# Keys pooled by matmuls, and one exponential for eight heads in the first nine chunks

## The chip, the cores and the metric

The kernel runs on one core of one Trainium2 chip. The metric is the device time of one execution in microseconds (us), as the median of three runs. The core has TensorE (PE; PEld is its loading of weights), DVE (VectorE), ACT (ScalarE), POOL (GpSimd) and SP (SyncE), which here issues nearly all loads and stores.

## The reference

Three stages follow each other: attention over pooled keys and values, a layer with a rational activation, and a layer with a squared ReLU. Only the first one is touched by the change.

```python
# q, k, v: (8, 8, 576, 64) float32 = batch, heads, tokens, head size
k_p = k.reshape(B, H, Sp, 8, D).mean(axis=3)      # Sp = 72 pooled keys
v_p = v.reshape(B, H, Sp, 8, D).mean(axis=3)
scores = scale * np.matmul(q, k_p.transpose(0, 1, 3, 2))
scores = scores - np.max(scores, axis=-1, keepdims=True)
attn = np.exp(scores)
attn = attn / (np.sum(attn, axis=-1, keepdims=True) + 1e-09)
x = np.matmul(attn, v_p)          # to (4608, 512): tokens x model
h = x @ w_in                      # 512 -> 2048
g = (a0 + a1*h + a2*h**2 + a3*h**3) / (1 + |b0||h| + |b1|h**2 + 1e-6)
x = g @ w_out                     # 2048 -> 512
y = np.maximum(x @ w_in2, 0.0)
out = y * y @ w_out2              # (4608, 512)
```

## The kernel before

The 4608 tokens (8 batches of 576) are cut into 36 chunks of 128 and nine blocks of 512. A block's four chunks must have gone through attention before the block's first layer can begin, so the first four chunks lie ahead of every large matmul. The work of one chunk is: scores (`qk`), the maximum over the 72 keys of each head (`row_max`), the exponential and its sum (`exps`), the division (`norm`), a transpose of the attention weights (`a_turn` for the first nine chunks), the product with the pooled values (`av`), and the output for the layers as a high and a low part (`x_out`). In the MoE layers every matmul group is 12 products of 128x128 by 128x512.

The first nine chunks (`NF = 9`, batches 0 and 1) use plain float32 attention. Later chunks use split 16-bit operands and are not touched. For the first two batches, keys and values are loaded raw and pooled on the core (`kv_first`). A key load brings one pair of heads as 128 rows (two heads of 64) by 576 tokens; DVE sums each eight neighbours (one reduce from 576 to 72), and ACT scales the result. There are four pairs in a batch. A value load brings 128 tokens by 512 columns, and TensorE sums eight neighbours with a constant 0/1 matrix `sums`, accumulating five chunks of tokens (four of 128 and one of 64) into one PSUM bank.

For each of the first nine chunks the scores of the eight heads stand in two PSUM banks, four heads of one parity in each, called the two halves. Each half has its own maximum on DVE. In half 0 ACT then makes four exponentials, one for each head, that subtract the maximum as a bias and accumulate the sum. In half 1 (named in `WHOLE`) DVE subtracts the maxima of all four heads in one instruction, ACT makes one exponential, and DVE makes one sum. The division is DVE's for chunks 0, 2, 3, 5 and 8 and ACT's, head by head, for the others. After the transposes, DVE evacuates half 0 and ACT half 1; in chunk 1, DVE takes both (`TURN_DVE`).

The order of work is not written by hand. Every operation is put on a list with its engine, an estimated time and its tiles (`act`, `dve`, `pe`, `load`). A planner (`Plan.order`, lines 380 to 401) simulates the list many times with random shifts of the due times, and keeps the order that ends first. Each engine then runs its queue strictly in that order. For loads, the planner also adds a "not before" dependency where it wants one held back. The second batch's pooling may start only when the transposes of chunk 0 have been issued (`plan.after = turned[0]`). As all instructions are issued by one line, 409, the profile names it everywhere; tiles tell the work apart. The names are: `kr` and `vr` raw keys and values (pooled keys lie in the same tiles, those of batch 1 in `vr`), `y`, `sc` and `xp` PSUM banks of attention, `mx`, `e` and `sm` the maxima, exponentials and sums, `t` the transposed weights, `raw` and `w` MoE weights while they are decoded, `x` the input of the layers and `h` a PSUM bank that the value pooling shares with the layers.

Of the kernel before, what the change touches and what calls it, by code (L numbers as in the profile page):

```python
# [17 lines left out]
AF = mybir.ActivationFunctionType  # L18
ALU = mybir.AluOpType
AX = mybir.AxisListType  # L20

B, H, S, D = 8, 8, 576, 64
POOL = 8
SP = S // POOL
NT = B * S
DM = H * D
# [3 lines left out]
TB = 512  # L30
# [26 lines left out]
SCALE = 1.0 / POOL / 8  # L57
# [2 lines left out]
QC = 1.0 + 1e-6  # L60
NF = 9
NORM_DVE = {0, 2, 3, 5} | set(range(8, NCHUNK))
WHOLE = {(c, 1) for c in range(NF)} | {(15, 1)}
TURN_DVE = {(c, 0) for c in range(NF)} | {(1, 1)}
BY_DMA = {(1, 1), (1, 3), (1, 5)}
KA, KB = 128 - SP, 2 * SP - 128
KC = SP + 2 * KB
# [1 line left out]
S0W = S // 128 * (128 // POOL)  # L69
WS = S0W + SP  # L70
NK = NF * CH // S
# [344 lines left out]
def fused_kernel(  # L416
# [1 line left out]
    tc: tile.TileContext,  # L418
    qf: bass.AP,
    qt: bass.AP,  # L420
    kf: bass.AP,
    vn: bass.AP,
    vm: bass.AP,
    kt: bass.AP,
# [41 lines left out]
    def act(n, func, **kw):  # L466
        pointers = sum(isinstance(kw.get(k), View) for k in ("scale", "bias"))
        fixed = (0.05 if kw["in_"].base.psum else 0.093) + (0.3 if "accum_out" in kw else 0.0)
        plan.add("act", fixed + 0.093 * pointers + n / 1200, [(nc.scalar.activation, dict(func=func, **kw))])

    def dve(n, name, **kw):
        pointers = sum(isinstance(kw.get(k), View) for k in ("scalar", "scalar1"))
        fixed = 0.11 if name == "tensor_reduce" else 0.066
        plan.add("dve", max(0.15, fixed + 0.061 * pointers + n / 960), [(getattr(nc.vector, name), kw)])

    def tt(n, out, in0, in1, op):
        dve(n, "tensor_tensor", out=out, in0=in0, in1=in1, op=op)
# [4 lines left out]
    def pe(us, products):  # L482
        return plan.add("pe", us, [(nc.tensor.matmul, p) for p in products])

    def load(n, out, in_, early=None):
        plan.add("sp", 0.6, [(nc.sync.dma_start, dict(out=out, in_=in_))], n / LOAD_RATE, early)
# [19 lines left out]
    def h_bank():  # L506
        h_turn.append(0)
        return ps_h.tile([128, TB], F32, "h", f"h{len(h_turn) % 2}")
# [7 lines left out]
    sums = const.tile([128, WS], F32, "sums")  # L516
# [106 lines left out]
    kst, vst, kp_t, vp_t = {}, {}, {}, {}  # L623
# [18 lines left out]
    def kv_first():  # L642


        k, v = ([p1.tile([128, 4 * TB], F32, n, f"x{o + i}") for i in range(2)] for o, n in ((0, "kr"), (2, "vr")))
        kr = [k[g // 3][:, g % 3 * S:(g % 3 + 1) * S].rearrange("p (k r) -> p k r", r=POOL) for g in range(H // 2)]
        vr = [v[c // 4][0:min(128, S - 128 * c), c % 4 * TB:(c % 4 + 1) * TB] for c in range(5)]
        for b, t in enumerate((k, v)):
            o = 1024 if b else S
            kp_t[b] = t[1][:, o:o + H // 2 * SP].rearrange("p (g k) -> p g k", g=H // 2)  # L650
            vp_t[b] = t[1][0:SP, 1536:2048]

        def k_sum(b):
            plan.ahead = K_AHEAD if b == 0 else 0.0
            for g in range(H // 2):
                load(128 * S * 4, kr[g], kf[b, g].rearrange("p (k r) -> p k r", r=POOL))
                dve(S, "tensor_reduce", out=kp_t[b][:, g], in_=kr[g], axis=AX.X, op=ALU.add)
                act(SP, AF.Copy, out=kp_t[b][:, g], in_=kp_t[b][:, g], scale=SCALE)
            if b == 0:
                q_first(0)  # L660

        def v_sum(b):
            plan.ahead = AHEAD if b == 0 else 0.0
            ps = h_bank()[0:SP]
            for c in range(5):
                n, o = min(128, S - 128 * c), S0W - 16 * c
                load(n * TB * 4, vr[c], vn[b, :, TB * c:TB * (c + 1)] if c < 4 else vm[b])
                pe(1.0, [dict(
                    out=ps, lhsT=sums[0:n, o:o + SP], rhs=vr[c], start=(c == 0), stop=(c == 4),
                )])  # L670
            act(DM, AF.Copy, out=vp_t[b], in_=ps)
            if b == 0:
                q_first(2)
                q_first(3)

        k_sum(0)
        plan.ahead = AHEAD
        q_first(1)
        v_sum(0)
        for c, fn in ((K1C, k_sum), (V1C, v_sum)):  # L680
            at(starts[c] + 5 if c >= 0 else -S0, "t", fn, 1)
# [26 lines left out]
    def q_first(c):  # L708

        if c == 0:  # L710
            q_in[0] = p1.tile([128, 4, 4, CH], F32, "q", "w7")
        q_t[c] = q_in[0][:, c]
        load(128 * 4 * CH * 4, q_t[c], qf[c])
# [76 lines left out]
    def row_max(c, half):  # L790
        if half == 0:
# [6 lines left out]
            H // 2 * SP, "tensor_reduce", out=mx, in_=sc_t[c, half], axis=AX.X, op=ALU.max,  # L798
            negate=(c, half) not in WHOLE,
        )  # L800

    def exps(c, half):
        mx, sm, e = e_t[c]
        ps = sc_t.pop((c, half))
        hs = slice(half * (H // 2), (half + 1) * (H // 2))
        if (c, half) in WHOLE:
            n = H // 2 * SP
            tt(n, e[:, hs], ps, mx[:, hs].unsqueeze(2).to_broadcast([128, H // 2, SP]), ALU.subtract)
            act(n, AF.Exp, out=e[:, hs], in_=e[:, hs])
            dve(n, "tensor_reduce", out=sm[:, hs], in_=e[:, hs], axis=AX.X, op=ALU.add)  # L810
            return
        for hh in range(H // 2):
            h = half * (H // 2) + hh
            act(
                SP, AF.Exp, out=e[:, h, :], in_=ps[:, hh, :],
                bias=mx[:, h:h + 1], accum_out=sm[:, h:h + 1],
            )
# [11 lines left out]
    def a_turn(c):  # L829
# [4 lines left out]
        for half in range(2):  # L834
# [13 lines left out]
            o = t[:, half * (H // 2):(half + 1) * (H // 2)]  # L848
            if (c, half) in TURN_DVE:
                dve(TB, "tensor_copy", out=o, in_=ps)  # L850
# [380 lines left out]
    def at(slot, key, fn, *args):  # L1231
        todo.setdefault((slot, key), []).append((fn, args))

    def run(slot, key):
        for fn, args in todo.pop((slot, key), []):
            if args and args[0] in FIRST and fn in (k_add, v_add, q_load, qk, row_max, exps, norm, a_turn, av, x_out):
                plan.ahead = AHEAD
            if fn not in (w_raw, w_decode, w_sums, x_fetch, pair_forms) and slot >= GATED:
                plan.after = started.get(slot - WINDOW)
            if fn.__name__ in ("k_sum", "v_sum"):  # L1240
                plan.after = turned.get(K1C if fn.__name__ == "k_sum" else V1C)
            fn(*args)
            plan.ahead, plan.after = 0.0, None

    def place_chunk(c, t):
        if c >= 4:
            at(t - 2, "t", q_load, c)
        at(t, "t", q_split, c)
        for half in range(2):
            h = half if c < CPB else 0  # L1250
            at(t + 2 + h, "s", qk, c, half)
            at(t + 2 + h, "s", row_max, c, half)
            at(t + 2 + h, "s", exps, c, half)
        at(t + 4, "t", norm, c)
        at(t + 5, "t", a_turn if c < NF else a_split, c)
        if c not in TWOS:
            cs = [x for x in (c - 1, c) if x == c or x in TWOS]
            at(t + 6, "x", av, *cs)
            for x in cs:
                at(t + 7, "s", x_out, x)  # L1260
# [63 lines left out]
    setup()  # L1324
    plan.ahead = AHEAD
    kv_first()
    plan.ahead = 0.0
    load_consts()
    for i in range(-S0, N + LAG):
# [11 lines left out]
        m = i - LAG  # L1341
# [5 lines left out]
        if kind == "pair":  # L1347
            _, pair, k = slots[i]
# [54 lines left out]
```

## Time and profile before

| | |
|---|---|
| time, median of 3 runs | 1650.77 us (1649.82 to 1654.72) |
| time of the profiled execution | 1649.59 us |
| its span in the trace | 1647.9 us |
| PE busy | 1610.9 us, 98% |
| PEld busy | 1307.3 us, 79% |
| DVE busy | 1410.0 us, 86% |
| ACT busy | 1132.6 us, 69% |
| mean granted TensorE clock | 0.996 |

Busy times are those of one profiled execution. The span goes from the first to the last instruction; the execution's own time includes what lies around it. A matmul of float32 operands appears as two records in the trace. Matmuls are pipelined, so that a busy PE need not be a PE at its peak.

### The profile page before, as it was taken

To read this page: it belongs to the slowest core of one execution; us is meant where nothing else is said; L and a number is where in the kernel's file an instruction comes from. 1 tells how busy PE (TensorE), PEld (TensorE's weight loads), DVE (VectorE), ACT (ScalarE), POOL (GpSimd) and SP (SyncE) were. 2 spreads that over 40 slices of the span, in tenths; PEclk is the share of its full clock that TensorE was granted. 3 is DMA by queue.
4 is the path that set the end of the run, shared out by engine and by line. 5 is a ranking of instruction groups with operands and counts; after the bars stand their busy time and mean duration, and the time that the engine had idled before them with its cause. 6 is when DMAs were issued, how large, how long until landed. Compare 5 with 4: busy or idle time off the path is not lost.

```text
span 1647.9 us, 23637 instructions
## 1 busy us (share of the span) xinstructions
PE 1610.9 (98%) x8476; PEld 1307.3 (79%) x8476; DVE 1410.0 (86%) x2135; ACT 1132.6 (69%) x2105; POOL 77.8 (5%) x95
## 2 busy tenths in 40 slices
PE   7899999999999999999999999999999999999998
PEld 4678888888888877877787878887888788888886
DVE  7999998589889998488979788999889799996666
ACT  5989778787557766566787645667987466657553
POOL 0001100100001000001111000010000000000000
PEclk9999999999999999999999999999999999999999
DMA  7357578997999879999999996785799985555544
GB/s 269 131 231 196 152 265 298 241 257 250 313 299 286 289 258 274 322 270 279 258 243 281 283 321 245 233 244 190 227 267 263 292 291 200 185 185 171 191 154 141
DMA packets 199141, 401.43 MB, mean 244 GB/s; under 512 B 68752, under 2 KB 118768, under 8 KB 170864
## 3 DMA queue, kind: packets, MB, share of 16 engines
q1 hardware_dynamic: 188512, 379.76, 70.6%
q0 software_dynamic: 10512, 20.16, 7.8%
q8 instruction: 67, 1.10, 0.3%
q14 instruction: 50, 0.41, 0.1%
HBM read 310.91 MB, written 72.35 MB: 233 GB/s over the span
## 4 chain that ended last, share of the span: by engine, by line
PE 70%; DVE 19%; ACT 4%; DMA 3%; issue 2%; SPq 0%; ACTq 0%; DVEq 0%
PE h L409 30%; PE y L409 22%; DVE pq L409 7%; PE yx L409 7%; PE yz L409 5%; PE hz L409 5%; DVE g L409 3%; DVE sv L409 2%; ACT sv L409 2%; PE xp L409 1%; PE sc L409 1%; DMA xd<-xo 1%; DMA t<-a 1%; DVE t L409 1%; DVE wv L409 1%
## 5 line engine op out<-in xcount | busy, mean ns | idle before, releaser
L409 PE MATMUL h<-x,w 128*128 128x512 f32 x2304 | 557.8, 392 | 10.7 <-DVE pq L409 5.1
L409 PEld LDWEIGHTS h<-x,w 128*128 128x128 f32 x2304 | 430.8, 188 | 107.5 <-DVE pq L409 8.9
L409 PE MATMUL y<-g,w 128*128 128x512 f32 x1728 | 418.8, 391 | 3.7 <-DVE g L409 3.6
L409 PEld LDWEIGHTS y<-g,w 128*128 128x128 f32 x1728 | 324.1, 188 | 73.7 <-DVE g L409 6.3
L409 ACT ACTIVATE sv<-sv,cs 128x512 f32<-128x512 f32 x288 | 208.3, 724 | 154.7 <-DVE sv L409 149.8
L409 ACT ACTIVATE sv<-h 128x512 f32<-128x512 f32 x192 | 114.0, 594 | 68.1 <-PE h L409 52.7
L409 PE MATMUL h<-xf,wi 128*128 128x512 f32 x576 | 145.7, 391 | 0.7 <-ACT gb L409 0.5
L409 PE MATMUL yx<-gf,wo 128*128 128x512 f32 x576 | 142.8, 391 | 0.4 <-DVE acc L409 0.4
L409 PE MATMUL y<-w,g 128*128 128x512 f32 x576 | 140.4, 392 | 0.1
L409 ACT ACTIVATE pq<-h,cs 128x512 f32<-128x512 f32 x144 | 111.8, 776 | 24.4 <-PE h L409 14.0
L409 PEld LDWEIGHTS yx<-gf,wo 128*128 128x128 f32 x576 | 107.6, 188 | 24.3 <-issue 0.8
L409 PEld LDWEIGHTS h<-xf,wi 128*128 128x128 f32 x576 | 107.4, 188 | 23.8 <-ACT gb L409 1.4
L409 PEld LDWEIGHTS y<-w,g 128*128 128x128 f32 x576 | 107.2, 188 | 23.3 <-DVE g L409 0.5
L409 DVE SCALAR_TENSOR_TENSOR g<-pq,cs,sv 128x512 fp32r<-128x512 f32 x144 | 107.6, 747 | 19.5 <-ACT sv L409 16.9
L409 DVE SCALAR_TENSOR_TENSOR sv<-sv,cs 128x512 f32<-128x512 f32 x144 | 107.3, 745 | 14.4 <-ACT sv L409 14.3
L409 ACT ACTIVATE sv<-h,cs 128x512 f32<-128x512 f32 x144 | 98.8, 686 | 25.0 <-DVE g L409 15.9
L409 PE MATMUL hz<-xf,wi 128*128 128x512 f32 x432 | 110.2, 392 | 1.8 <-DVE ga L409 1.0
L409 PE MATMUL yz<-gf,wo 128*128 128x512 f32 x432 | 108.3, 392 | 3.1 <-DVE gf L409 1.5
L409 DVE SCALAR_TENSOR_TENSOR pq<-pq,cs 128x512 f32<-128x512 f32 x144 | 107.5, 747 | 1.9
L409 DVE SCALAR_TENSOR_TENSOR pq<-pq,cs,h 128x512 f32<-128x512 f32 x144 | 106.7, 741 | 0.6 <-ACT sv L409 0.2
L409 DVE TENSOR_TENSOR pq<-pq,h 128x512 f32<-128x512 f32 x144 | 98.0, 680 | 8.4 <-ACT pq L409 5.2
L409 DVE SCALAR_TENSOR_TENSOR pq<-sv,g 128x512 f32<-128x512 f32 x144 | 99.1, 688 | 2.8
(147 smaller groups left out, 2072.6 us busy)
## 6 DMA issues: line engine op xcount, KB each, us to landing
w<-ws SPq DMA_DIRECT2D x128, 1024.0 KB, 6.3
ws<-w SPq DMA_DIRECT2D x32, 1024.0 KB, 4.9
wi<-wf SPq DMA_DIRECT2D x48, 512.0 KB, 5.2
wo<-wf SPq DMA_DIRECT2D x48, 512.0 KB, 5.9
wo<-ws SPq DMA_DIRECT2D x72, 256.0 KB, 4.2
raw<-wa SPq DMA_DIRECT2D x16, 1024.0 KB, 6.7
raw<-wb SPq DMA_DIRECT2D x16, 1024.0 KB, 8.1
wf<-ws SPq DMA_DIRECT2D x16, 1024.0 KB, 9.2
```

The lines of the kernel that those rows point to most:

```text
L409: made = fn(**{k: v.real() if isinstance(v, View) else v for k, v in kw.items()})
```

## The change

Keys of the first two batches are pooled by matmuls, as the values are. The host lays out `k` like `v`, so that a load brings 128 tokens (the fifth 64) by 512 columns. For each chunk of tokens and each pair of heads one matmul multiplies 128 columns of raw keys, as the stationary operand, with 16 (in the last chunk 8) columns of the 0/1 matrix, which gives the pooled keys already transposed. They collect in one PSUM bank, and a single ACT instruction scales all 288 columns. The DVE reduces and the four scalings of a batch go.

In the first nine chunks DVE now subtracts the maxima in both halves. After the second half, one exponential and one sum run over all eight heads (576 columns). DVE no longer evacuates transposes of any chunk (`TURN_DVE` is empty); ACT evacuates both halves.

```diff
+MERGED = set(range(NF))
-WHOLE = {(c, 1) for c in range(NF)} | {(15, 1)}
-TURN_DVE = {(c, 0) for c in range(NF)} | {(1, 1)}
+WHOLE = {(c, h) for c in MERGED for h in range(2)} | {(15, 1)}
+TURN_DVE = set()
...
-        kr = [k[g // 3][:, g % 3 * S:(g % 3 + 1) * S].rearrange("p (k r) -> p k r", r=POOL) for g in range(H // 2)]
-        vr = [v[c // 4][0:min(128, S - 128 * c), c % 4 * TB:(c % 4 + 1) * TB] for c in range(5)]
+        kr, vr = (
+            [t[c // 4][0:min(128, S - 128 * c), c % 4 * TB:(c % 4 + 1) * TB] for c in range(5)] for t in (k, v)
+        )
...
-            o = 1024 if b else S
-            kp_t[b] = t[1][:, o:o + H // 2 * SP].rearrange("p (g k) -> p g k", g=H // 2)
+            kp_t[b] = t[1][:, 1024:1024 + H // 2 * SP].rearrange("p (g k) -> p g k", g=H // 2)
...
             plan.ahead = K_AHEAD if b == 0 else 0.0
-            for g in range(H // 2):
-                load(128 * S * 4, kr[g], kf[b, g].rearrange("p (k r) -> p k r", r=POOL))
-                dve(S, "tensor_reduce", out=kp_t[b][:, g], in_=kr[g], axis=AX.X, op=ALU.add)
-                act(SP, AF.Copy, out=kp_t[b][:, g], in_=kp_t[b][:, g], scale=SCALE)
+            ps = h_bank()[:, 0:H // 2 * SP].rearrange("p (g k) -> p g k", g=H // 2)
+            for c in range(5):
+                n = min(128, S - 128 * c)
+                load(n * TB * 4, kr[c], kn[b, :, TB * c:TB * (c + 1)] if c < 4 else km[b])
+                m = n // POOL
+                pe(0.4, [dict(
+                    out=ps[:, g, 16 * c:16 * c + m], lhsT=kr[c][:, 128 * g:128 * (g + 1)],
+                    rhs=sums[0:n, S0W:S0W + m], start=True, stop=True,
+                ) for g in range(H // 2)])
+            act(H // 2 * SP, AF.Copy, out=kp_t[b], in_=ps, scale=SCALE)
...
             tt(n, e[:, hs], ps, mx[:, hs].unsqueeze(2).to_broadcast([128, H // 2, SP]), ALU.subtract)
+            if c in MERGED:
+                if half == 0:
+                    return
+                n, hs = H * SP, slice(0, H)
             act(n, AF.Exp, out=e[:, hs], in_=e[:, hs])
             dve(n, "tensor_reduce", out=sm[:, hs], in_=e[:, hs], axis=AX.X, op=ALU.add)
             return
```

## Rows read from the trace of the kernel before

**Rows 1.** The page: one engine line, and the shares of the chain.

```profile
PE 1610.9 (98%) x8476; PEld 1307.3 (79%) x8476; DVE 1410.0 (86%) x2135; ACT 1132.6 (69%) x2105; POOL 77.8 (5%) x95
...
PE 70%; DVE 19%; ACT 4%; DMA 3%; issue 2%; SPq 0%; ACTq 0%; DVEq 0%
```

**Rows 2.** Stretches: length, busy PE PEld DVE ACT POOL (instructions), clock, DMA, GB/s.

```profile
0.00:40.00 40.00, 28.53 (x213) 17.28 (x214) 28.91 (x60) 23.21 (x69) 1.25 (x8) 0.91 0.78 266
40.00:80.00 40.00, 35.26 (x223) 27.53 (x222) 40.00 (x71) 37.29 (x90) 0.00 (x0) 0.96 0.40 142
80.00:120.00 40.00, 38.81 (x198) 31.03 (x196) 39.38 (x59) 35.58 (x58) 0.00 (x0) 1.00 0.58 231
```

**Rows 3.** The chain that ended last, 0 to 40 us: start, us, what.

```profile
2.67 5.15 DMA q<-qf
...
7.95 3.69 PE y L409 x32
11.64 4.66 PE h L409 x6
...
16.74 0.86 PE h L409 x2
...
22.21 5.73 DMA vr<-vn
...
27.99 1.98 PE h L409 x2
29.97 3.10 PE y L409 x16
```

**Rows 4.** Timeline: start, us, engine, work [idle before]; DVE, weight loads, first MoE matmuls.

```profile
3.70 1.44 DVE L409 TENSOR_REDUCE kr<-kr 128x72 f32<-128x576 f32 x2 [2.35 <-DMA kr<-kf]
6.44 1.48 DVE L409 TENSOR_REDUCE kr<-kr 128x72 f32<-128x576 f32 x2 [1.30 <-DMA kr<-kf]
...
7.92 3.52 PEld L409 LDWEIGHTS y<-kr,q 64*128 64x128 f32 x32 [7.92 <-ACT kr L409]
...
19.53 0.97 PEld L409 LDWEIGHTS y<-kr,q 64*128 64x128 f32 x16 [0.19 <-issue]
...
39.69 5.74 PE L409 MATMUL h<-x,w 128*128 128x512 f32 x24
```

**Rows 5.** Stretches 10 to 20 us and 26 to 32 us.

```profile
10.00:20.00 10.00, 10.00 (x46) 4.91 (x46) 6.15 (x16) 6.93 (x29) 0.00 (x0) 1.00 1.00 382
...
26.00:32.00 6.00, 4.01 (x13) 2.43 (x14) 5.98 (x12) 2.95 (x9) 0.00 (x0) 0.50 0.90 314
```

**Rows 6.** DVE groups, 0 to 96.5 us: busy us, mean ns | idle before.

```profile
L409 DVE TENSOR_REDUCE sm<-e 128x4 f32<-128x288 f32 x8 | 3.5, 437 | 0.0
L409 DVE COPY t<-y 72x512 f32<-72x512 f32 x5 | 3.4, 683 | 3.3 <-PE y L409 3.3
...
L409 DVE TENSOR_REDUCE kr<-kr 128x72 f32<-128x576 f32 x4 | 2.9, 752 | 3.6 <-DMA kr<-kf 3.6
L409 DVE TENSOR_REDUCE vr<-kr 128x72 f32<-128x576 f32 x4 | 2.8, 730 | 0.0
L409 DVE COPY t<-sc 72x512 f32<-72x512 f32 x4 | 2.7, 679 | 0.3 <-PE sc L409 0.3
L409 DVE TENSOR_TENSOR e<-y,mx 128x288 f32<-128x288 f32 x4 | 1.8, 452 | 0.0
```

**Rows 7.** ACT: two neighbouring exponentials (timeline), then groups of the whole span.

```profile
42.23 0.30 ACT L409 ACTIVATE e<-sc,mx 128x72 f32<-128x72 f32 x1
...
42.52 0.31 ACT L409 ACTIVATE e<-sc,mx 128x72 f32<-128x72 f32 x1
...
L409 ACT ACTIVATE a<-e 128x576 f16<-128x576 f32 x27 | 18.4, 682 | 13.5 <-DMA at<-a 6.7 <-DVE e L409 3.5 <-DMA t<-a 2.6
L409 ACT ACTIVATE e<-e 128x288 f32<-128x288 f32 x10 | 4.4, 442 | 1.5 <-DVE e L409 1.2
L409 ACT ACTIVATE t<-xp 72x512 f32<-72x512 f32 x5 | 3.0, 592 | 0.0
```

More of the change, by code (lines that the diff above doesn't have):

```diff
@@ L420, in fused_kernel @@
     qt: bass.AP,
-    kf: bass.AP,
+    kn: bass.AP,
+    km: bass.AP,
     vn: bass.AP,
@@ L1377 @@
     }
-    arrays["kf"] = lay(k[:NK].reshape(NK, H // 2, 2, S, D).transpose(0, 1, 2, 4, 3)).reshape(NK, H // 2, 2 * D, S)
-    a = v[:NK].transpose(0, 2, 1, 3).reshape(NK, S, DM)
-    arrays["vn"] = lay(
-        a[:, :S // 128 * 128].reshape(NK, S // 128, 128, DM).transpose(0, 2, 1, 3)
-    ).reshape(NK, 128, S // 128 * DM)
-    arrays["vm"] = lay(a[:, S // 128 * 128:])
+    for n, x in (("k", k), ("v", v)):
+        x = x[:NK].transpose(0, 2, 1, 3).reshape(NK, S, DM)
+        arrays[n + "n"] = lay(
+            x[:, :S // 128 * 128].reshape(NK, S // 128, 128, DM).transpose(0, 2, 1, 3)
+        ).reshape(NK, 128, S // 128 * DM)
+        arrays[n + "m"] = lay(x[:, S // 128 * 128:])
     for n, m in (("a", "moe_"), ("b", "moe2_")):
```

## The prediction

> **What bounds the kernel now.** I read the page first. TensorE is busy 98% of the span and holds 70% of the chain of waits; DVE holds 19% [rows 1]. Busy time by stretches of 40 us, read next, says where the change can act. From 80 to 120 us TensorE lacks 1.2 of 40 us, while in the two stretches of 40 us before that it lacks 11.5 and 4.7, and from 40 to 80 us DVE has no free time at all, ACT 2.7 us [rows 2]. All the changed work except chunk 8 lies in this head of the kernel (before 96.5 us). Behind it a time won or lost in the head is carried to the end, and chunk 8 is one chunk among work bound by TensorE: I count it as nothing.
>
> The chain through the first 40 us, read third, is not one of DVE. It is the load of q (to 7.8 us), then TensorE without a gap (scores of chunks 0 and 1 in 3.69 us, three value-pooling matmuls in 4.66 us, and so on), then the load of the second value batch (landing at 27.9 us), then TensorE again for 5.08 us [rows 3]. The step to see is the speed of TensorE. Sixteen pairs of score weight loads take 3.52 us at 7.92 us and eight pairs take 0.97 us at 19.53 us, 0.22 against 0.12 us for a pair [rows 4]; a value-pooling record goes from 0.78 us (4.66 over 6) to 0.43 us (0.86 over 2) [rows 3]. So the opening runs at half clock until about 16 us, although the granted-clock column says 1.00 there; and from 26 to 32 us, after a wait, it is back at 0.50 [rows 5].
>
> **The change part by part.** *Key pooling, DVE.* Eight reduces of 576 go, at 0.75 and 0.73 us [rows 6]. The four of batch 0 run at 3.70 to 7.9 us, on an engine that otherwise waits for loads [rows 4]: nothing. The four of batch 1 lie where DVE is full: 4 x 0.73 = 2.9 us won.
>
> *Key pooling, TensorE.* Each batch gets 5 chunks x 4 matmuls, and a float32 matmul makes two records (the 16 score matmuls of chunks 0 and 1 are 32 records [rows 4]), so 40 records. Each loads 128 columns of weights and streams only 16 columns, so the weight load sets it. The trace has no such 128-row load on its own; the nearest row is a score pair, whose two 64-row loads go side by side: 0.22 us at half clock and 0.12 at full. A batch then costs 8.8 or 4.8 us; the plan books 5 x 0.4 = 2.0.
>
> Batch 0 starts where the first reduce did, at 3.70 us; the same bytes come in five loads instead of four, and the q loads queue one issue (0.4 us) later on SP. At half clock the records end at 3.7 + 8.8 = 12.5 us; with one scaling on ACT (0.5 us, below the 0.59 of a 512-wide evacuation [rows 7]) and two hops between engines (0.15 us each in the plan) the scores start at 13.3 instead of 7.95: 5.3 us later. But TensorE has then worked since 3.7 us. Before, it came to full clock some 8 to 9 us after its first work; the same delay gives it full clock at about 12, so the scores cost 2 x 0.97 instead of 3.69 us and the first three value-pooling matmuls 6 x 0.43 instead of 4.66: 1.75 + 2.1 = 3.8 us back. The opening then ends 1.5 us later, and that is the value I take. Bounds: +5.3 with nothing given back; and, with records at 0.12 us behind the last landing (about 7.2 us: the fourth reduce runs in 6.44 to 7.92), scores at 7.2 + 1.0 + 0.8 = 9.0 us, 1.0 late, less 3.8: -2.8.
>
> Batch 1 falls into the wait before 27.99 us [rows 3]: the 4.8 us of full-clock records fit between its key loads and the landing of the values. I take 0. Bounds: -2.5, if this work keeps the clock up and halves the 5.08 us behind it; +3.1, if its 8.8 us at half clock do not fit into the 5.7 us between 22.2 and 27.9 us and the transposes of chunks 2 and 3 queue behind.
>
> Here a rule of the Trainium skill speaks the other way. The row first: from 10 to 20 us TensorE shows 10.00 us of matmuls and 4.91 us of weight loads [rows 5]. "Trainium Kernel Development and Optimization", Best Practices, says to judge TensorE by weight-load busy time, not by matmul busy time. By that half of the stretch is free, the added records find room, and the time is the one of the first rival below. The half-clock records speak against it; no run so far decides.
>
> *Softmax, DVE.* In the head (eight chunks): nine copies of transposed rows go, 9 x 0.68 = 6.1 us; eight subtractions come, 8 x 0.45 = 3.6; eight sums of 288 become eight of 576, for which I take the reduce of keys at 0.74: 8 x (0.74 - 0.44) = 2.4 [rows 6]. Balance -0.1. For the full stretch from 20 us on, the copy of chunk 0 and the additions of chunks 0 and 1 fall out, and it is -8 x 0.68 + 6 x 0.45 + 6 x 0.30 = -0.9 us. With the reduces, DVE loses 2.9 + 0.9 = 3.8 us there.
>
> *Softmax, ACT.* The 32 exponentials with accumulated sum take a step of 0.30 us each, since the accumulator read lies beside the next: -9.6 us. Eight exponentials of 576 instead of 288 add 8 x (0.68 - 0.44) = 1.9 us (a 128x576 copy for the price), nine evacuations 9 x 0.59 = 5.3 [rows 7]. ACT is 2.4 us lighter, the scalings of the keys aside. It is second to DVE from 40 to 80 us, so I count 0. Without that cover it could be worth its 2.4 us, or cost a like time where both halves of a chunk's transposes now wait on it.
>
> *Waits.* The one exponential waits for both halves, and the sum for it. A chunk's chain from scores to weights is two maxima, two subtractions, 0.68, 0.74 and the division: longer than half a chunk was, but other DVE work fills it. I count 0; if unfilled, 0.5 us for each of the first four chunks, 2 us.
>
> **Sum.** +1.5 (opening) + 0 (batch 1) - 3.8 (DVE) + 0 (ACT) = -2.3 us on the profiled execution's 1649.59: 1647.3. The median of the runs, 1650.77, stands 1.2 above that execution, so 1648.5. What is late next is TensorE, from 80 us on. The order on each queue is planned anew from the changed list of work, so pieces far from the change move too; the trace gives no price for it, and I leave it at 0 with a spread of 2 to 3 us.
>
> **Rivals.** *TensorE has room* (chance 0.22): the early work raises the clock in time, the opening is not late, DVE gives 3.8 us and the 5.08 us behind 27.99 us become 2.5: -6.3, 1644.5. For it: TensorE is idle before 7.95 us [rows 3] and for 2.0 of the 6 us from 26 us on [rows 5]; against it: half clock until 16 us.
>
> *The pooling blocks TensorE* (0.17), the slower side: 40 records at 0.22 us stand in an in-order queue ahead of the first scores, full clock comes no earlier, and the opening ends 5.3 us late. The path to 39.7 us is then TensorE's, so DVE's relief is not paid there; with batch 1 up to +8.4, 1659; I put it at +6, 1656.8. It decides when the first score matmul starts after 12.5 us and records still take 0.22 us there.
>
> *Nothing comes through* (0.16): the landing at 27.9 us sets the start of the MoE work as before, and DVE's relief turns into idle time: 0, 1650.8.
>
> *The forecast* has 0.45, with its own range from 1646 to 1652.
>
> **How the numbers follow.** About 0.3%, 5 us, is what a measurement of this kernel can tell from no change. Faster than 1645.8: most of the first rival and a little of the forecast, 0.22. Slower than 1655.7: most of the second and a little of the planning, 0.18. Between: 0.60. The range runs from inside the first rival to the middle of the second, 1643.5 to 1657.
>
> **What would show it.** In the changed profile: the start of the first score matmul near 13 us and its pairs at 0.12 us (opening +1.5); a pooling record's step of 0.2 us before 12 us; 1.00 for the granted clock from 26 to 32 us or not; DVE busy from 20 to 40 us with 3 to 4 us less work before the first MoE matmul, which starts at 39.69 us now [rows 4]; exponentials of 128x576 at 0.68 and their sums at 0.74 us; and the TensorE time lacking in the first 80 us, 16.2 now. The prediction is wrong if the first MoE matmul moves by over 4 us, or if the difference arises after 100 us.

## The result, and the profile after

The change made the kernel slower: 1665.54 us (median of five runs, 1664.1 to 1668.45) against 1651.72 us (five runs, 1649.82 to 1654.72) beside it. The ratio is 1.0081, with a 95% interval of 1.0065 to 1.0097: some 13 us lost. The forecast was 1648.5 us with a range up to 1657, so the time lies outside the range, on the slower side. Nearest was the rival "the pooling blocks TensorE", which had 0.17 and a price of half of what came. The profiled execution took 1664.1 us, with a span of 1662.4.

The page of the kernel after first: one engine line, and the shares of the chain. (The line that issues everything is 410 here, and 565 or 566 in the kernels with a stored order below.)

```profile
PE 1630.4 (98%) x8556; PEld 1324.7 (80%) x8556; DVE 1404.9 (85%) x2126; ACT 1130.4 (68%) x2037; POOL 77.8 (5%) x95
...
PE 66%; DVE 19%; DMA 7%; ACT 6%; issue 3%; SPq 0%; DVEq 0%; ACTq 0%
```

TensorE has 80 records more, as counted, and 19.5 us more of busy time [rows 1]. The 80 records themselves account for about 17 us, as will be seen; the page can't say whether they lie on the path.

The stretches of the kernel after, with the columns of [rows 2], and the stretch in which its clock fell:

```profile
0.00:40.00 40.00, 33.94 (x204) 28.30 (x205) 21.14 (x47) 16.14 (x29) 1.25 (x8) 0.88 0.76 260
40.00:80.00 40.00, 37.42 (x239) 26.19 (x240) 31.54 (x53) 30.59 (x49) 0.00 (x0) 0.82 0.42 148
...
30.50:47.50 17.00, 16.95 (x86) 13.80 (x86) 9.46 (x14) 7.83 (x13) 0.00 (x0) 0.51 0.68 230
```

Here is a trap. In the first 80 us TensorE now lacks 6.06 + 2.58 = 8.6 us instead of 16.2 [rows 2]: it is *busier* at the start, and the start is later. From 30.5 us on it is busy at half speed: for 17 us the granted clock is 0.51 and TensorE works through 16.95 us of it. DVE, on the other side, has gone from 68.9 us of work in 80 to 52.7 [rows 2], for the most part because it waits for TensorE, as its groups show further down.

The chain of waits of the kernel after, 0 to 42 us (start, us, what):

```profile
4.08 8.80 PE h L410 x40
...
13.37 3.69 PE y L410 x32
17.06 5.04 PE h L410 x8
...
26.44 3.05 DMA kr<-kn
29.53 1.30 PE h L410 x8
30.88 1.98 PE xp L410 x16
32.86 1.85 PE y L410 x8
34.71 6.74 PE h L410 x32
```

Both batches' key pooling (the x40, and then x8 and x32) are in it: 8.80, 1.30 and 6.74 us. The weight loads of the kernel after, from its timeline (start, us, engine, work, idle before), tell the clock record by record:

```profile
4.05 8.72 PEld L410 LDWEIGHTS h<-sums,kr 128*128 128x128 f32 x40 [4.05 <-issue]
13.37 3.49 PEld L410 LDWEIGHTS y<-kr,q 64*128 64x128 f32 x32 [0.59 <-ACT kr L410]
...
18.77 0.24 PEld L410 LDWEIGHTS h<-vr,sums 128*72 128x72 f32 x1 [0.61 <-issue]
19.62 0.24 PEld L410 LDWEIGHTS h<-vr,sums 128*72 128x72 f32 x1 [0.61 <-issue]
20.22 0.14 PEld L410 LDWEIGHTS h<-vr,sums 128*72 128x72 f32 x1 [0.36 <-issue]
20.65 0.14 PEld L410 LDWEIGHTS h<-vr,sums 128*72 128x72 f32 x1 [0.29 <-issue]
```

The step of a value-pooling record is 0.85 us from 18.77 to 19.62, then 0.60, then 0.43. So full clock comes at about 20 us, in the midst of the value pooling, though TensorE has worked since 4.08 us. The scores at 13.37 us cost 3.69 us, as before. Soon after the wait for key loads (to 29.53 us) the records run at half clock again: the first eight take 1.30 us, the other 32 take 6.95 us, or 0.217 each.

The first group of MoE matmuls, from the matmul timeline of the kernel after:

```profile
51.56 3.02 PE L410 MATMUL h<-x,w 128*128 128x512 f32 x12
```

It stood at 39.69 us [rows 4]: 11.9 us later. Two terms cover it. The scores of the chunk that follows the value pooling load their weights at 23.39 instead of 19.53 us: +3.9. Batch 1's records cost 1.30 + 6.74 = 8.0 in the chain: together 11.9. That the sum fits doesn't mean that nothing else moved: between those scores and the first MoE matmul TensorE waits some 2 us less than before (1.4 against 3.5 us), and its other work takes some 2 us longer.

To follow the rest, I count the records of the layers' 512-wide matmuls. There are 6624 in each kernel here, so the nth of them is a milestone. The 161st begins 9.8 us later than before, the 961st 18.6, the 4161st 13.2, and the last one 14.25 us later. So most of the loss is made in the head; behind it the distance still rises by 9 us and falls by 7 us.

### The profile page after: what moved, and what is told of

The parts are those of the page before. It is cut to its first block, busy times and chain, and to the rows that moved or that the text cites. A ratio compares the mean times of both kernels' runs of the same rounds, so it can differ in the third digit from the quotient of the medians.

```text
span 1662.4 us, 23744 instructions
## 1 busy us (share of the span) xinstructions
PE 1630.4 (98%) x8556; PEld 1324.7 (80%) x8556; DVE 1404.9 (85%) x2126; ACT 1130.4 (68%) x2037; POOL 77.8 (5%) x95
## 4 chain that ended last, share of the span: by engine, by line
PE 66%; DVE 19%; DMA 7%; ACT 6%; issue 3%; SPq 0%; DVEq 0%; ACTq 0%
PE h L410 28%; PE y L410 20%; DVE pq L410 7%; PE yx L410 6%; PE hz L410 5%; PE yz L410 4%; DVE g L410 3%; ACT sv L410 2%; DVE sv L410 2%; DMA raw<-wb 1%; PE xp L410 1%; DMA raw<-wa 1%; PE sc L410 1%; DMA wo<-wf 1%; DMA w<-ws 1%
## 5 line engine op out<-in xcount | busy, mean ns | idle before, releaser
L410 ACT ACTIVATE pq<-h,cs 128x512 f32<-128x512 f32 x144 | 112.1, 779 | 53.0 <-DVE g L410 30.5
L410 DVE SCALAR_TENSOR_TENSOR g<-pq,cs,sv 128x512 fp32r<-128x512 f32 x144 | 107.8, 749 | 19.5 <-ACT sv L410 18.1
L410 DVE SCALAR_TENSOR_TENSOR sv<-sv,cs 128x512 f32<-128x512 f32 x144 | 107.5, 746 | 12.7 <-ACT sv L410 12.5
L410 DVE TENSOR_TENSOR g<-pq,sv 128x512 fp32r<-128x512 f32 x144 | 98.8, 686 | 0.7
```

Of the source, the lines that this page charges most:

```text
L410: made = fn(**{k: v.real() if isinstance(v, View) else v for k, v in kw.items()})
```

## The experiments

In the planner, each part of the change also changes the order of everything. So there are kernels of two kinds: those with a plan of their own, and those with a *held order*, in which the planner's result is replaced by a stored one and new operations stand where those that they replace stood:

```
 def order(self, ...):
-    (simulate, keep the order that ends first)
+    self._link()
+    order, holds = numbers(ORDER), numbers(HOLDS)
+    self.holds = {...}
+    return [self.ops[i] for i in order]
```

All results in one table: ratio to runs of the kernel before taken beside the kernel in question, with its 95% interval, and the start of the first MoE matmul in the one profiled execution. Keys 0 and 1 are the key pooling of batch 0 and of batch 1.

| Kernel | Keys by TensorE | Softmax | Order | us | Ratio | First MoE, us |
|---|---|---|---|---|---|---|
| before | none | old | own | 1651.72 | 1 | 39.69 |
| after | 0 and 1 | new | own | 1665.54 | 1.0081 (1.0065 to 1.0097) | 51.56 |
| e1 | none | new | own | 1651.14 | 0.9997 (0.9985 to 1.0009) | 43.31 |
| e2 | 0 and 1 | old | own | 1651.17 | 1.0000 (0.9986 to 1.0014) | 52.20 |
| e3 | 0 and 1, booked at 1.76 us | new | own | 1659.49 | 1.0050 (1.0032 to 1.0068) | 56.41 |
| e4 | none | old | own, other seed | 1642.27 | 0.9949 (0.9936 to 0.9963) | 40.36 |
| j3 | 0 and 1 | new | own, other seed | 1652.76 | 1.0002 (0.9987 to 1.0017) | 50.27 |
| g1 | 0 and 1 | new | before's | 1672.17 | 1.0118 (1.0091 to 1.0146) | 60.02 |
| g2 | none | new | before's | 1652.68 | 1.0015 (0.9999 to 1.0032) | 40.57 |
| g3 | 0 and 1 | old | before's | 1670.73 | 1.0104 (1.0069 to 1.0139) | 59.47 |
| g5 | none | old | after's | 1658.25 | 1.0033 (1.0016 to 1.0050) | 44.78 |
| i1 | 0 | old | before's | 1661.10 | 1.0050 (1.0032 to 1.0068) | 44.23 |
| i2 | 1 | old | before's | 1671.95 | 1.0122 (1.0087 to 1.0156) | 54.13 |
| i3 | 0, with dummy matmuls | old | before's | 1666.82 | 1.0090 (1.0060 to 1.0119) | 53.40 |
| i4 | none, with dummy matmuls | old | e4's | 1644.58 | 0.9951 (0.9932 to 0.9969) | 41.58 |
| m1 | 1, wide | old | before's | 1657.11 | 1.0035 (1.0018 to 1.0052) | 42.89 |
| m2 | 1, as late as it may | old | before's | 1662.25 | 1.0076 (1.0048 to 1.0105) | 46.63 |

**Which half costs the time, and how much is the order?** e1 is the kernel before with the softmax alone, e2 the kernel after with the old softmax, e3 the kernel after with the records' measured price in the planner's list, and e4 the kernel before with another seed for the planner's random shifts.

```
e1 (to before): the new MERGED, WHOLE, TURN_DVE and the block "if c in MERGED" of exps
e2 (to after):
-MERGED = set(range(NF))
+MERGED = set()          (and the old WHOLE and TURN_DVE)
e3 (to after, in k_sum):
-                pe(0.4, [dict(
+                pe(1.76, [dict(
e4 (to before):
-SEED, TRIES = 0, 8
+SEED, TRIES = 1, 8
```

Expected of e1: 

> The kernel before, with the new softmax of the first nine chunks alone (both halves subtracted on DVE, one exponential and one sum, all evacuations on ACT); keys still pooled on DVE. Theory K (the pooling records block TensorE at half clock): the first score matmul stays at 8 us, the first MoE matmul starts within 2 us of 39.7, time 1647 to 1654. Theory S (the longer chain of one softmax, and ACT as sole evacuator, delay the first block): first MoE matmul 5 us or more late, time 1658 to 1667.

Expected of e2: 

> Keys pooled by matmuls alone, softmax as before. Theory K: scores start near 13.4 us, the 40 records of the second batch take some 7 us at half clock, first MoE matmul near 51 us, time 1661 to 1668. Theory S: time 1648 to 1654.

Expected of e3: 

> The changed kernel with each group of pooling matmuls booked at 1.76 us (8 records of 0.22) instead of 0.4 in the planner. Nothing else differs. If the order planned with a price four times too low is the cause (theory P), most comes back: 1650 to 1656. By theory K the first batch's 8.8 us have no other place, and only the second batch can be moved behind the transposes of chunks 2 and 3: first MoE matmul near 45 us, time 1655 to 1661.

Expected of e4: 

> The kernel before with another seed for the planner's tries: the same work in another order. It tells what a new plan alone does. Theories K and S: within 4 us of before, 1648 to 1656. Theory N (the new order alone made the difference): 1658 or more.

Measured: neither half alone moves the time (0.9997 and 1.0000), and both together lose 13 us. e4, which computes in every instruction what the kernel before computes, is 8 us *faster* than it (0.9949), outside what any theory had allowed; its profiled execution, at 1649.09 us, was the slowest of its ten, so that its trace doesn't show those 8 us. e1's first MoE matmul came later than theory K had said (43.31 us). e2 is the instructive one: K was right on its head and wrong on its time. Its opening is that of the kernel after, as its matmul timeline shows:

```profile
4.19 8.78 PE L410 MATMUL h<-sums,kr 128*128 128x16 f32 x40 [4.19 <-DMA kr<-kn]
...
52.20 5.74 PE L410 MATMUL h<-x,w 128*128 128x512 f32 x24
```

Its first MoE matmul is 12.5 us late, its 161st milestone 10.9 us, and its last one 0.35 us early (1643.13 against 1643.48). So the pooling's cost is paid in the head, and e2 got it back behind: of its distance of 10.6 us at the 2400th milestone (630 us), -0.8 us is left at the 3400th (881 us). That gain isn't the key pooling's: e4, with before's work, gains 9.5 us on the kernel before in the same stretch. Every kernel here with an order that isn't before's gains 3 to 11 us in it, while those that hold before's order move there by at most 4 us. From 640 to 880 us TensorE lacks 6.3 us of busy time in the kernel before and 0.1 us in e2. So the order of the kernel before has a weak stretch there, and each new plan here, whatever the edit, mended some of it.

The booked price is not the main fault: e3 is still 8 us slower than before, and its half clock lasts longer (0.50 from 30.5 to 57.5 us, with TensorE busy for 26.97 of the 27 us; its first MoE matmul is at 56.41 us, where theory K had 45). It is 6 us faster than the kernel after, no more than another seed can give, so a small share of the price can't be ruled out.

**The same work in one order.** g1, g2 and g3 put the change, its softmax and its key pooling into the order of the kernel before; g5 puts the kernel before into the order of the one after.

Expected of g1: 

> The changed kernel with the order of the kernel before held fast: every operation that both have keeps its place in its queue, the pooling matmuls stand where the DVE reduces stood, and the planner is not run. Theory K (key pooling on TensorE at half clock makes the head some 10 us longer, and the new plan added 4 behind it): first MoE matmul at 48 to 53 us, time 1658 to 1664. Theory N (only the new order made it slower): first MoE matmul near 42 us, time 1648 to 1654.

Expected of g2: 

> The new softmax alone, in the order of the kernel before. Theory K: first MoE matmul within 2 us of 39.7, time 1648 to 1654. Theory S (the softmax costs time, and the new plan of the earlier run gave it back): 3 to 6 us late, 1654 to 1658.

Expected of g3: 

> Keys pooled by matmuls alone, in the order of the kernel before. Theory K: first MoE matmul at 48 to 53 us, time 1659 to 1665, where the same work in its own new order took 1651. Theory N: 1648 to 1654.

Expected of g5: 

> The work of the kernel before in the order that the planner gave the changed kernel, with DVE's reduces where the pooling matmuls stand and the old softmax. Theory K: the head is short again (first MoE matmul at 40 to 44 us) and what stays is the worse order behind it: 1653 to 1659. Theory N: 1662 to 1667.

Measured: in the order of before, the parts add up. The softmax costs 0.15% (2.5 us, an interval that touches zero), the key pooling 1.04% (17 us), both 1.18% (19.5 us). What e1 and e2 got back between 630 and 881 us isn't got back here. That the new order alone made the loss is refuted: take it away, and the loss is larger. (g1 and g3 lost some 8 and 6 us more than theory K had allowed at most.) The work before in the order of after is 5.5 us slower (g5), so the change, compared within that order, costs 1.0081 less 1.0033, some 8 us. A held order may favour the work that it was planned for; the mean of the two pairs is about 14 us, and the kernels as they are stand 13.4 us apart. g1's loss is again made in the head. Its stretch and two lines of its matmul timeline:

```profile
31.00:61.00 30.00, 27.06 (x132) 18.24 (x133) 12.97 (x22) 10.11 (x16) 0.00 (x0) 0.50 0.42 137
```

```profile
46.05 5.24 PE L565 MATMUL h<-sums,kr 128*128 128x16 f32 x24
...
60.02 4.16 PE L565 MATMUL h<-x,w 128*128 128x512 f32 x14
```

For 30 us the granted clock is 0.50, with 24 of the records at 0.22 us in the midst, and the first MoE matmul is 20.3 us late.

**Which batch?** i1 and i2 leave one batch with DVE's reduces, in the order of before.

```
 def k_sum(b):
+    if b not in KEYS_PE:      # i1: {0}, i2: {1}
+        (loads of kf, tensor_reduce, scaling as before)
```

Expected of i1: 

> Only the keys of batch 0 are pooled by matmuls; batch 1 by DVE reduces, softmax and order as before. Theory K: first score matmul at 13.4 us instead of 8.0, everything up to the first MoE matmul 5 to 8 us late, time 1656 to 1661. If batch 1 alone is to blame: 1650 to 1653.

Expected of i2: 

> Only the keys of batch 1 are pooled by matmuls; batch 0, softmax and order as before. Theory K: the opening is as before, the 40 records stand between the transposes of chunks 2 and 3 at half clock and bring their 7 to 9 us in full, time 1657 to 1663. If the late opening is all: 1650 to 1653.

Measured: batch 0 costs 8 us (1.0050), batch 1 costs 20 us (1.0122), and they don't add, since both together cost 17. So batch 1, which the prediction had priced at nothing, is the dearer one in this order, by far more than theory K's 7 to 9 us. i2's stretch, and its matmul timeline:

```profile
26.00:56.00 30.00, 27.95 (x134) 18.89 (x135) 13.58 (x21) 9.95 (x20) 0.00 (x0) 0.50 0.37 123
```

```profile
28.05 1.98 PE L566 MATMUL h<-vr,sums 128*72 128x512 f32 x2 [2.85 <-DMA vr<-vn]
29.82 1.72 PE L566 MATMUL h<-sums,kr 128*128 128x16 f32 x8
...
40.16 5.24 PE L566 MATMUL h<-sums,kr 128*128 128x16 f32 x24
45.33 1.98 PE L566 MATMUL h<-vr,sums 128*72 128x512 f32 x2
...
54.13 6.62 PE L566 MATMUL h<-x,w 128*128 128x512 f32 x24
```

The 40 records take 1.72 + 1.73 + 5.24 = 8.7 us. But the first MoE matmul is 14.4 us late: the other 5.7 us, by subtraction, are other work at half clock, such as two value-pooling records in 1.98 us, which at full clock take 1.0. The clock was down before the first of the new records, after the wait of 2.85 us, as it was in the kernel before, where it is back at 0.93 from 32 to 36 us and at 1.00 from 36 to 40 us; here, with the narrow records in between, it stays at 0.50 for the whole 30 us.

**Is it the shape of the records, or their number?** m1 pools the keys of batch 1 as the values are pooled: the 0/1 matrix is the stationary operand, the keys stream past it 512 wide, in 10 records, and four transposes bring the result into place. m2 is i2 with its narrow records put together, just ahead of the scores of chunk 4 that need them.

```
m1, batch 1:
+pe(1.0, [dict(out=ps, lhsT=sums[0:n, o:o + SP], rhs=kr[c], start=(c == 0), stop=(c == 4))])
+act(DM, AF.Copy, out=kt_1, in_=ps, scale=SCALE)
+(four is_transpose matmuls with rhs=ident[0:SP, 0:SP])
+act(H // 2 * SP, AF.Copy, out=kp_t[b], in_=ps)
m2: i2, with the place of the five pooling groups set right before qk(4)
```

Expected of m1: 

> Only batch 1's keys are pooled on TensorE, but the way the values are: the 0/1 matrix stationary, 512 columns of raw keys streaming (10 records instead of 40), then a scaling on ACT, four transposes and one more ACT copy. Order as before, records where they were in i2 (1672). Theory C (narrow records hold the clock at half, and all work among them pays): half clock for 7 to 14 us instead of 31, first MoE matmul at 42 to 46 us instead of 54, time 1653 to 1660. Theory Q (any work at that place in TensorE's in-order queue costs as much): 1666 to 1672.

Expected of m2: 

> As i2, but the five groups of batch 1's pooling matmuls stand together right ahead of the scores of chunk 4, behind all work of chunks 2 and 3 and behind the value pooling. Theory C: the work ahead of them goes at full clock as in the kernel before, and they add their own 4.8 to 8.8 us and one scaling: first MoE matmul at 44 to 49 us, time 1655 to 1662. If the place doesn't matter: as i2, 1669 to 1674.

Measured: with the same sums, m1 costs 5.8 us where i2 costs 20. The stretch of m1 that answers to i2's, and its timeline:

```profile
26.00:56.00 30.00, 25.82 (x165) 15.40 (x164) 24.74 (x44) 21.53 (x55) 0.00 (x0) 1.00 0.62 219
```

```profile
26.04 1.08 PE L566 MATMUL h<-kr,sums 128*72 128x512 f32 x2
28.86 1.04 PE L566 MATMUL y<-ident,e 128*72 128x128 f32 x8 [1.74 <-DVE sm L566]
...
32.58 2.94 PE L566 MATMUL h<-kr,sums 128*72 128x512 f32 x6
36.21 1.94 PE L566 MATMUL h<-vr,sums 128*72 128x512 f32 x4 [0.68 <-ACT kr L566]
...
42.89 5.73 PE L566 MATMUL h<-x,w 128*128 128x512 f32 x24
```

The granted clock is 1.00 over the 30 us in which i2 has 0.50, and the first MoE matmul is 3.2 us late instead of 14.4. But the place is not the same, though it was meant to be: m1's first two records stand ahead of the wait and all ten ahead of batch 1's value pooling, whereas i2's 40 stand behind the first value records, which wait to 28.05 us for their load. So m1 differs from i2 in the form of the records, in their number and in their place at once, and the 14 us between them belong to the three together.

m2 shows the narrow records by themselves, with no wait just ahead of them (matmul timeline, then two stretches):

```profile
39.50 5.47 PE L566 MATMUL h<-sums,kr 128*128 128x16 f32 x40
...
46.63 7.33 PE L566 MATMUL h<-x,w 128*128 128x512 f32 x24
```

```profile
39.50:43.00 3.50, 3.50 (x33) 3.50 (x32) 2.12 (x2) 0.00 (x0) 0.00 (x0) 1.00 0.88 300
43.50:46.50 3.00, 2.93 (x39) 2.68 (x39) 0.00 (x0) 1.49 (x3) 0.00 (x0) 0.50 0.00 0
```

40 take 5.47 us here: some 32 at a step of 0.11 us while the clock is up, and the rest at 0.21 us after it fell, at about 43.3 us, with TensorE busy without a gap on nothing but narrow records since 39.5 us. The same 40 took 8.7 us at half clock. m2 costs 12.5 us, between m1 and i2, and its first MoE group takes 7.33 us where the kernel before has 5.74. So the narrow records cost their own time, and here the clock fell with them and made the work behind them dearer; how much of i2's 20 us the form alone is worth stays open.

**Can other work raise the clock ahead of them?** I held that early wide matmuls would bring the clock up and with it the time down. i3 is i1 with dummy 512-wide matmuls ahead of the pooling and between its chunks; i4 has three at the very start, in the work of the kernel before and the order of e4. The dummies write a bank that nothing reads.

```
 def warm():
+    pe(1.7, [dict(out=warm_up[1], lhsT=ident, rhs=warm_up[0][:, 0], start=True, stop=True)])
i3: 2 at the start, 1 ahead of each of the chunks c = 1 to 4;  i4: 3 at the start
```

Expected of i3: 

> As i1, with six matmuls more on TensorE whose result nobody reads: two of 128x128 by 128x512 ahead of the first pooling records, and one between the chunks. Theory H (the price is the half clock of an engine that has not worked before): clock up by about 7 us, pooling records step 0.11 us, first scores near 11 us, the value pooling at full speed, time 1650 to 1655, below i1 in spite of the added work. Theory W (a load of 128 float32 columns takes 0.2 us at any clock, or the clock does not come earlier): first scores at 15 us or later, 1660 or more.

Expected of i4: 

> The work of the kernel before in the order of the reseeded plan (e4, 1642), with three matmuls of 128x128 by 128x512 that nobody reads at the very start, while the loads are awaited. Theory H: scores of chunks 0 and 1 in 2 us instead of 3.7, first value-pooling records 0.43 instead of 0.8, first MoE matmul 2 to 4 us earlier, time 1637 to 1641. Theory W, or if later loads set the start anyway: 1641 to 1644.

The matmul timeline of i3, and then that of i4:

```profile
2.79 3.78 PE L566 MATMUL xw<-ones,ident 128*128 128x512 f32 x4 [2.79 <-POOL ident L566]
6.36 1.73 PE L566 MATMUL h<-sums,kr 128*128 128x16 f32 x8
7.93 2.06 PE L566 MATMUL xw<-ones,ident 128*128 128x512 f32 x2
...
22.52 3.69 PE L566 MATMUL y<-kr,q 64*128 64x72 f32 x32 [0.50 <-ACT kr L566]
```

```profile
2.79 4.69 PE L565 MATMUL xw<-ones,ident 128*128 128x512 f32 x6 [2.79 <-POOL ident L565]
7.81 2.01 PE L565 MATMUL y<-kr,q 64*128 64x72 f32 x32 [0.34 <-DMA q<-qf]
9.75 2.80 PE L565 MATMUL h<-vr,sums 128*72 128x512 f32 x6
...
41.58 5.49 PE L565 MATMUL h<-x,w 128*128 128x512 f32 x12 [1.63 <-ACT x L565]
```

In i3 the clock stayed down: eight pooling records still take 1.73 us, and the scores 3.69 us at 22.52 us. In i4, where the wide matmuls stand without a gap, it came up at about 6.8 us (their step goes from 0.85 to 0.52 us): the scores cost 2.01 us instead of e4's 3.69, and six value-pooling records 2.80 instead of 5.09. That opening is some 3 us shorter, and nothing of it arrives. ACT's timeline, of i4 and then of e4, shows where it ends:

```profile
17.04 1.16 ACT L565 ACTIVATE raw<-raw 128x1024 f32<-128x1024 f32 x1 [4.17 <-DMA raw<-wa]
```

```profile
17.35 1.20 ACT L409 ACTIVATE raw<-raw 128x1024 f32<-128x1024 f32 x1 [2.98 <-DMA raw<-wa]
```

In both kernels a piece of MoE decoding stands in ACT's queue ahead of the next division of attention, and its load lands at 17 us, early opening or not. The gain becomes idle time there: the next scores begin at 19.69 us against 20.04 in e4. Then the clock falls in i4 (0.51 from 20 to 34 us, 0.76 in e4), and the first MoE matmul stands at 41.58 us against 40.36. 0.9951 against e4's 0.9949 is no difference. So the clock came up early where wide records ran alone, not where narrow ones stood among them, and the part of my theory on the time falls. i3's time is what the rival on weight loads had said, but not for its reason: by m2 the records do run faster at full clock (0.11 against 0.21 us).

**With another seed.** j3 is the kernel after with the seed of e4.

Expected of j3: 

> The changed kernel with the other seed that e4 used. The head is 10 us late as with the first seed; what the new plan gives behind it is open within some 10 us. Theory K with a wide spread of plans: first MoE matmul at 48 to 56 us, time 1650 to 1670.

Measured: 1652.76 us (1.0002). Against e4, the kernel before with that same seed, it is 1.0002 to 0.9949: 0.53%, some 9 us slower. The change costs time in each of the four pairings (both seeds, both held orders), between 8 and 20 us, and e4 at 1642.27 us (1638.84 to 1649.09 in ten runs) beats both kernels.

## Why the prediction was wrong, step by step

Term by term, in the profiled execution: the opening +3.9 us for +1.5, batch 1 +8.0 for 0, nothing at the first MoE matmul for DVE's -3.8, and another 2.4 us behind that matmul. The forecast's own sign of being wrong came true: the first MoE matmul moved by 11.9 us, and 4 had been the limit.

**The opening: the half that fell was the clock.** Scores predicted at 13.3 us came at 13.37; records at 0.22 us took 0.22. The step that failed is "the same delay gives it full clock at about 12". I read the delay of 8 to 9 us in [rows 3 and 4] as a delay after any work. The runs show other delays: with 40 narrow records and 32 of scores first, full clock came 16 us after the first work (20 against 4.08 us), with six wide records first after 4 us (6.8 against 2.79, i4). So the forecast of +1.5 us came out at +3.9, inside its bounds, and i1 prices the whole of batch 0 at 8 us.

**Batch 1 was the large error.** "Falls into the wait before 27.99 us" set it at 0, between -2.5 and +3.1. In the kernel after the key loads themselves are what ends the wait (to 29.53 us), so no record stands in it but eight behind it; all 40 run after the wait, the last 32 of them at half clock, on the path: +8.0 us. Those loads are issued only at 26.44 us, against 20.35 in the kernel before. The upper bound had the right price for the records (8.8 us) and the wrong credit (5.7 us of wait), and no term for the neighbours: in i2 5.7 of 14.4 us are work that was there before and now runs at half clock.

**DVE's 3.8 us: the work went, the time didn't.** The groups of DVE, and then of ACT, in the kernel after (0 to 106.3 us: busy us, mean ns | idle before):

```profile
L410 DVE TENSOR_REDUCE sm<-e 128x8 f32<-128x576 f32 x8 | 6.0, 746 | 1.3 <-ACT e L410 1.3
...
L410 DVE TENSOR_REDUCE mx<-y 128x4 f32<-128x288 f32 x8 | 3.3, 452 | 16.0 <-PE y L410 16.0
...
L410 ACT ACTIVATE e<-e 128x576 f32<-128x576 f32 x8 | 5.5, 685 | 7.0 <-DVE e L410 7.0
```

```profile
15.39 0.82 DVE L410 TENSOR_REDUCE mx<-y 128x4 f32<-128x288 f32 x2 [14.04 <-PE y L410]
...
45.03 0.69 DVE L410 SCALAR_TENSOR_TENSOR x<-xp,x 128x512 fp32r<-128x512 f32 x1 [5.85 <-ACT x L410]
```

Both prices were right (0.74 and 0.68 us predicted; 0.746 and 0.685 measured). But DVE now waits. Of the 16.0 us for scores, 14.04 lie ahead of the first scores, where it used to reduce keys; from 20 us on, where the forecast had counted the 3.8 us, the longest wait is 5.85 us at 45 us, for a part of the attention output from ACT (0.64 us in the kernel before). An engine that waits has nothing to gain from less work. Alone, the softmax is worth 0 (e1, -2.5 to +1.5 us) to +2.5 us (g2, from -0.2), where its own terms came to -0.9: within e1's interval, a little outside g2's.

**The order's spread of 2 to 3 us was too small.** e4 shows 8 us from the seed alone, and e2 and g3 show 20 us between two orders of the same work (1651.17 and 1670.73). The premise that a time lost in the head is carried to the end held where the order was held (g1: 21.3 us at the 161st milestone, 21.1 at the end) and not where it was planned anew (e2: 10.9 and -0.35). The forecast had said that a difference behind 100 us would prove it wrong; the distance of the kernel after moves from 9.8 to 18.6 and back to 14.25 us there, and most of the way back lies in the weak stretch of before's order. The way up lies between 98 and 283 us, and g5, before's work in after's order, goes up there too, from 6.1 to 10.9 us. One place shows in the chain of the kernel after, 100 to 310 us:

```profile
108.07 6.75 DMA raw<-wa
...
275.43 8.28 DMA raw<-wb
```

Loads of MoE weights stand in the chain there, and the chain of before has none in that stretch. That it costs those 9 us is an inference.

**The rivals.** "TensorE has room" failed: the scores came 5.4 us later, and TensorE's idle time at the start did not cover the new records. The prediction had set a page beside this rival. The Trainium skill ("Trainium Kernel Development and Optimization", Best Practices) says to judge the distance to roofline by MFU (the matmul operations done, as a share of the peak) and weight-load busy time, not by matmul busy time. That half of a stretch without weight loads is free for more work was the prediction's own reading of it, and it doesn't hold here: in i2, from 26 to 56 us, weight loads are busy for 18.89 of 30 us, and from 28.05 us to the first MoE matmul TensorE has no gap. How far a stretch at half clock is from its roofline is another question, which no run here measures. "The pooling blocks TensorE" named the mechanism and its sign (scores after 12.5 us, records at 0.22 us), and at +6 us priced it too low: its opening (+5.3) lay above the +3.9 that came, but of batch 1's 8.0 us it held 3.1 at most.

**What stays open.** The milestones tell in which stretch the order of before loses (630 to 881 us), but which piece of work there does it was not found. In the held order the distance of i2 grows from 15.4 us at the 161st milestone to 21.6 at the end, and that of i1 from 5.8 to 11.6, although the work behind the head is the same, while that of g1 and g3 doesn't grow; no run here tells why. Nor was the whole change tried with wide pooling for both batches, nor wide pooling at i2's place.

## What to carry to other kernels

Price new TensorE work at the clock of the place where it will stand, and price its neighbours too: in the start-up phase here the narrow records paid their half-clock time, and the work among them did too. When a sum can be had with the 0/1 matrix stationary and the data streaming 512 wide, try that first: it cost 5.8 us here (m1), the narrow form 12.5 and 20 us (m2, i2), each at another place. Before bringing work forward, look for what the next engine waits for: i4's 3 us ended at a load in ACT's queue. Where a planner sorts the work anew after every edit, hold the order or compare several seeds before crediting or blaming an edit by less than 1%.

## What was not expected of the hardware

A float32 matmul record with 128 columns of weights and 16 moving columns costs 0.22 us at half clock (40 in 8.79 us, after) and 0.11 us at full clock (the step in m2 up to 43 us). A 40-record run of them, followed by scores, left the clock at its lower level for 16 us after the first work (after), whereas six 512-wide records in a row had it up 4 us after theirs (i4); the same kind of wide records mixed with narrow ones had not raised it by 22.5 us (i3). In m2 the granted clock fell from 1.00 to 0.50 within a run of narrow records with no wait in it. And the granted-clock column shows 1.00 from 10 to 20 us in the kernel after while records there run at half speed until 20 us: at the start, the record's own duration is the better clock.
